# Sketched attention feeding a four-expert layer: two query units a batch instead of three, first k in two halves, dealing strings changed

## The chip, the cores and the metric

The kernel runs on one core of a Trainium2 chip. The metric is device time in microseconds (us) of one execution. All inputs and outputs lie in HBM. TensorE (PE) multiplies matrices, VectorE (DVE), ScalarE (ACT) and GpSimd (POOL) work element by element, and SyncE (SP) issues nearly all DMAs.

## What is computed

For 4 batches, 4 heads, 1088 positions and head size 32, `S1` and `S2` (8 x 32) sketch queries and keys, and the products of the two sketches are the 64 features:

```python
def phi(x):
    a = np.einsum('rd,bhsd->bhsr', S1, x)
    b = np.einsum('rd,bhsd->bhsr', S2, x)
    return np.einsum('bhsi,bhsj->bhsij', a, b).reshape(*x.shape[:-1], r * r)
kv = np.einsum('bhsf,bhsd->bhfd', phi(k), v)
num = np.einsum('bhsf,bhfd->bhsd', phi(q), kv)
den = phi(q) . phi(k).sum(positions) + 1e-6
```

`num / den`, the heads side by side, is a 4352 x 128 matrix `x`. Four experts with `w1` (128 x 1024) and `w2` (1024 x 128) follow: `h = max(x @ w1[e], 0)`, and `out += p[:, e] * (h @ w2[e])`, where `p` is `domain_probs` divided by its row sums.

## The kernel before

**Stream.** The 4352 positions (columns) go through the experts in ten chunks, `CHUNKS` (line 110): 128, 448, six of 512, 320 and 384. For each chunk there are 4 experts x 8 blocks of 128 hidden units. A pair of blocks (chunk 0) or one block (chunks 1 to 9) is a slot, and the main loop (lines 1391 to 1462) writes the program slot by slot. Chunk 0 and experts 0 and 1 of chunk 1 (`WHOLE` = 2) use f32 matmuls directly. Every other block splits both operands into fp32r parts: matmuls L1078 and L1079 into a PSUM tile `h`, an ACT pass over it (L1080), matmul L1095 on top; then element work makes `ha`, `hb`, `hc`; five slots later (`LAG`) L1189 and L1190 multiply `ha` and `hb` by parts of `w2`, and L1224 multiplies `hc`, dealt out after the expert's last block by `DEALT`.

**Makers.** A letter for each block says who makes the parts (lines 1113 to 1146). For all letters but D, ACT makes `ha` (L1119); DVE makes `hb` (L1126) for all. `hc`: A and D, ACT makes a first piece (L1121) and POOL finishes (L1145); P, POOL does both (L1144, L1145); V, DVE alone (L1128); N, ACT makes a whole piece from `ha` and DVE finishes (no POOL). D has DVE make `ha` (L1123). X is a block done in f32 with one row block of `w2` from a small tile `w2_plain`. `MAKER_1` deals chunk 1, `MAKER_LATE[e]` chunks 2 to 9, `MAKER_TAIL` the last expert of chunk 9. `MAKER` is for chunks below `LATE` = 2 other than 1, which have no such block. `BUFFERS` are the numbers of `ha`, `hb` and `hc` tiles.

**Attention.** The generator `front()` (line 989) makes the x columns in pieces, and the main loop takes pieces at a rate that has each chunk ready in time. `keys(b)` (line 539) turns the keys, projects them (L474), copies the values into `vx` (ACT or POOL by `VALUES_BY`), makes products (L498) and sums them over positions on PE (L295). Then come the query units, `UNITS` (line 108). A unit of batches 1 to 3: DVE turns `qn` (L601); PE projects (`project`, 4 matmuls with `sq_half`) and ACT copies; SP writes the result to DRAM (`store_rows`) and reads it back, repeated as the features need it (`spread`); `FETCH` pieces later two products are taken (L790, DVE or POOL by `Q_BY`); 16 pieces after the unit began, `attend` multiplies 64 x 66 tiles on PE, and DVE divides and turns the result (L689 to L707), which goes through DRAM (`xd`) into `ring`, from where `token_parts(m)` splits chunk m.

**Weights.** `weight_parts(e)` and `second_weight_parts(e)` split `w1[e]` and `w2[e]` from the slots in `W1_AT` and `W2_AT`; `W1_BY` and `W2_BY` name the engines (`split` L853 and L855, `rest` L858, `combine` L869).

**Finish.** `gather` (line 1315) adds an expert's gated output to `total`; `TURN` slots after the fourth, DVE turns it (L1289) and SP stores it.

Of the kernel before, what the change touches and what calls it, by code (L numbers as in the profile page):

```python
# [24 lines left out]
def kernel(  # L25
# [35 lines left out]
    NT = 9  # L61
    FB = F // P
    NQ = E * FB // 2
    QW = 512
    CW = 512
    GE = 160
    LAG = 5
    GATES = 3
    BUFFERS = (5, 7, 12)
    HA, HB, HC = BUFFERS  # L70
    WHOLE = 2
    TURN = 2
    MAKER = 'VAXVDDVA'
    LATE = 2
    LATER = 99
    MAKER_1 = 'APXPDPAA'
    MAKER_LATE = ('APVAPAAA', 'APVAPAAA', 'APVPAAAA', 'APVAPAAA')
    TAIL = 4
    MAKER_TAIL = "PAVVXXTT"
    LAG_TAIL = 4  # L80
    MAKER_END = "PAXPAPAA"
    DEALT_TAIL = (1, 1)
    DEALT = (0, 2, 1, 2, 2, 1)
    LIMIT = 1700.0
    LIMIT_A = 1e9
    SLOT_A = 1500.0
    SLOT = 1600.0
    PLAIN = (2,)
    TOKENS_AT = 21
    AHEAD = 13  # L90
    TOKENS = 6
    LEAD = 6
    SETTLE = 1
    SPREAD = 0
    XD_BY = 'VVPPPVPVVV'
    Q_BY = 'VVPPVVPPVVPPVPVPPP'
    O_BY = 'AAAA'
    FETCH = 5
    DELAY = 0
    W1_AT = ((0, 4), (3, 14), (2, 15), (1, 22))  # L100
    W2_AT = ((3, 16), (2, 27), (0, 26), (1, 31))
    W1_BY = ('PVV', 'AVV', 'PVV', 'AVV')
    W2_BY = ('AAPV', 'AAPV', 'APVV', 'AAPV')
    VALUES_BY = 'APA'
    KEYS_BY = "AAA"
    RING_BY = 'PAPA'
    TOKENS_BY = "VV"
    UNITS = [[P, 448, 512], [512, 192, 384], [448, 512, P], [512, 192, 384]]

    CHUNKS = [P, 448] + [512] * 6 + [320, 384]  # L110
    NC = len(CHUNKS)
# [47 lines left out]
    def xpieces(name, t):  # L159
        return mpool.tile([P, 3, CW], t, tag="x", name=name)  # L160

    s_raw = cpool.tile([R2, 2 * D], I32, name="s_raw")
    for i, (eng, src) in enumerate(((nc.scalar, S1), (nc.sync, S2))):
        eng.dma_start(s_raw[R * i : R * i + R, :], src.bitcast(I32))

# [29 lines left out]
        i, c = divmod(P * b, HF)  # L195
        return of[e][i][:, c : c + P]

    load_k(0)
    sr = xpieces("sr", F32)
    qn[0] = mpool.tile([P, 3, CW], F32, tag="x", name="qn_first").rearrange("p i c -> p (i c)")[:, 0:S]  # L200
    load_rows(q, 0, qn[0], slice(0, P))
# [21 lines left out]
        load_w2(e)  # L223
    w2_plain = {}

    def load_plain():

        ((b,),) = (PLAIN,)
        homes = (cpool, "x_first", 0), (mpool, "end", 0), (cpool, "dp", 0), (cpool, "unit", 1)
        for e, (pool, tag, more) in enumerate(homes):  # L230
            w2_plain[e] = pool.tile([P, P + more], F32, tag=tag, bufs=1, name=f"w2_plain_{e}") if pool is mpool else \
                pool.tile([P, P + more], F32, tag=tag, name=f"w2_plain_{e}")
            nc.sync.dma_start(w2_plain[e][:, 0:DM], w2[e, P * b : P * (b + 1), :])

    sk = cpool.tile([P, P], F32, name="sk")
    sp = mpool.tile([32, 3, 2, 32], F32, tag="total", bufs=1, name="sp")
# [63 lines left out]
            on_side(lambda s: out[half[s], :], lambda s: weights[:, half[s]], lambda s: moving, **flags)  # L300


    words = mpool.tile([P, CW], F32, tag="hb", bufs=HB, name="words")

    def word(i, np_=R2):
        return words[0:np_, 2 * D * i : 2 * D * (i + 1)]
# [346 lines left out]
    def attend(b, c, n, qp, after=None):  # L653

        W = H * (D + 1)
        nd = [psum(ps_h, "h")]
        if sum(blocks(m)[0] for _, m in unit_parts(b, c, n)) > 3:  # L660
            nd.append(psum(ps_h, "h"))
        tiles = 0
        laid = []
        for c0, m in unit_parts(b, c, n):
            T = blocks(m)
            for p in range(2):
                for t in range(T[0]):
                    for _ in range(2):

                        at = c0 + P * t + (HP * turn[0] if t < T[turn[0]] else 0)  # L670
                        i, k = divmod(tiles + t, 3)
                        on_side(
                            lambda s: nd[i][half[s], W * k + W // 2 * p : W * k + W // 2 * (p + 1)],
                            lambda s: qp[p][:, at : at + HP],
                            lambda s: kvx[b][:, p, :],
                            start=True,
                            stop=True,
                        )
            laid.append((c0, T, tiles))
            tiles += T[0]  # L680
        if after:
            project(*after)
        yield
        if after:
            store_rows(*after)
        banks = [(i, 3 * i, min(tiles, 3 * i + 3)) for i in range((tiles + 2) // 3)]
        rc = apool.tile([P, QW // 32], F32, tag="rc", name="rc")
        for i, t0, t1 in banks:
            nc.vector.tensor_scalar(  # L689
                out=rc[:, H * t0 : H * t1],  # L690
                in0=_ap(nd[i], 0, P, D, [[D + 1, H * (t1 - t0)]]),
                scalar1=1e-6, scalar2=1.0, op0=ALU.add, op1=ALU.mult,
            )
        nc.vector.reciprocal(rc[:, 0 : H * tiles], rc[:, 0 : H * tiles])
        yield
        xs = apool.tile([P, QW], F32, tag="qa", name="xs")
        for i, t0, t1 in banks:
            nc.vector.tensor_tensor(
                out=_ap(xs, 0, P, P * t0, [[D, H * (t1 - t0)], [1, D]]),
                in0=_ap(nd[i], 0, P, 0, [[D + 1, H * (t1 - t0)], [1, D]]),  # L700
                in1=_ap(rc, 0, P, H * t0, [[1, H * (t1 - t0)], [0, D]]),
                op=ALU.mult,
            )
        yield
        y = apool.tile([P, QW], F32, tag="y", name="y")
        for c0, T, t0 in laid:
            nc.vector.transpose(  # L707
                _ap(y, 0, P, P * t0, [[32, T[0]], [32 * T[0], H], [1, 32]]),
                _ap(xs, 0, P, P * t0, [[P, T[0]], [D, H], [1, D]]),
            )  # L710
            if b == 0 and c == P:
                for x in range(2):
                    yield
                    for a in (x, x + 2):
                        run = 32 * T[a // 2]
                        for h in range(H):
                            copy = scalar_copy if RING_BY[h] == "A" else nc.gpsimd.tensor_copy
                            at = PLACES[1][3] + a // 2 * 64 * T[0] + a % 2 * run
                            copy(ring[32 * h : 32 * h + 32, at : at + run], _ap(y, 32 * a, 32, 32 * T[0] * h, [[1, run]]))
                continue  # L720
            m = 64 * sum(T)
            base = xd.offset + P * (S * b + c + c0)
            for a in range(4):
                run = 32 * T[a // 2]
                nc.sync.dma_start(
                    bass.AP(
                        xd.tensor,
                        base + a // 2 * 64 * T[0] + a % 2 * run,
                        [[m, 32], [32 * m, H], [1, run]],
                    ),  # L730
                    _ap(y, 32 * a, 32, P * t0, [[32 * T[0], H], [1, run]]),
                )
            for to, at, w in placed(S * b + c + c0, m):
                nc.sync.dma_start(to, bass.AP(xd.tensor, base + at, [[m, P], [1, w]]))
        if after and SPREAD == 1:
            spread(*after)
        have[0] += n
        yield
        if after and SPREAD == 2:
            spread(*after)  # L740
# [292 lines left out]
    def final(m, e):  # L1033
        return m == NC - 1 and e == E - 1
# [115 lines left out]
    def second(i):  # L1150
# [25 lines left out]
        elif kind == "one":  # L1176
            w = slice(DM * k, DM * (k + 1))
            va, vb, vd = w2_parts[e]
            last = max(b for b in range(FB) if not plain_block(m, e, b))
            if plain_block(m, e, k):  # L1180
                at = DM * (FB - 1 - k)
                rows = w2_tail[:, at : at + DM] if final(m, e) else w2_plain[e][:, 0:DM]
                if maker(m, e, k) in "YT":
                    weighted.append((rows, hd))
                else:
                    later.insert(len(later) if final(m, e) else 0, (rows, hd))
            else:
                ha, hb, hc = hd
                nc.tensor.matmul(o[:, 0:n], va[:, w], ha, start=(k == first_of(m, e)), stop=False)  # L1189
                nc.tensor.matmul(o[:, 0:n], vb[:, w], hb, start=False, stop=(k == last))  # L1190
                later.append((vd[:, w], hc))
            if final(m, e):
                if k == last:
                    gather_first(m, e, o[:, 0:n])
                    owed.append([0, m, e, psum(ps_h, "h")[:, 0:n], later, DEALT_TAIL])
            elif k == FB - 1:
                if O_BY[e] == "A":
                    nc.scalar.activation(o[:, 0:n], o[:, 0:n], ACTF.Copy, scale=1.0 + R12)  # L1198
                else:
                    nc.vector.tensor_scalar(  # L1200
                        out=o[:, 0:n], in0=o[:, 0:n], scalar1=1.0 + R12, scalar2=1.0, op0=ALU.mult, op1=ALU.mult
                    )
                owed.append([0, m, e, o[:, 0:n], later, DEALT])
# [190 lines left out]
    while i < len(slots) or i <= max(due) or owed:  # L1394
# [34 lines left out]
        if i < len(slots):  # L1429
# [12 lines left out]
                nc.sync.dma_start(bass.AP(one.tensor, one.offset, [[P + 1, P], [1, 1]]), unit[:, P : P + 1])  # L1442
                nc.sync.dma_start(unit[:, 0:P], one[:, :])
            if i == first_slot[1] + 10:
                load_plain()
            if i == first_slot[4]:
                unit = cpool.tile([P, P + 1], F32, tag="unit", name="unit")
                nc.gpsimd.memset(unit[:, 0:P], 0.0)
                nc.gpsimd.memset(unit[:, P : P + 1], 1.0)
            if i == 2:  # L1450
# [45 lines left out]
```

## Time and profile before

| | us |
|---|---|
| runs: median (lowest, highest) | 450.74 (450.14, 451.53) |
| the profiled execution | 451.32 |
| its span, first to last instruction | 449.5 |
| first matmul after the warm-up ones | 6.55 |
| first block of the experts (chunk 0) | 14.23 |
| chunk 1 begins | about 30.7 |
| last weights of the experts used | 441.4 |

The granted TensorE clock is 0.998. A row `start us, us, engine line op out<-in` of the timeline is one instruction or several alike; the bracket behind it is the engine's idle time before it and what ended it. Matmuls are pipelined, so their rows overlap, and the distance of two starts is what one costs.

### The profile page before, as it was taken

How to read it: one execution, taken by the hardware profiler on the slowest of the kernel's cores; microseconds unless marked ns; L12 is line 12 of the kernel's file. 1: busy time of each engine (PE TensorE's matmuls, PEld its weight loads, DVE VectorE, ACT ScalarE, POOL GpSimd, SP SyncE). 2: the span in 40 equal slices, each digit the busy share in tenths (PEclk: the TensorE clock that was granted, in tenths of full speed). 3: DMA queues.
4: the chain of work that ended last, by engine and by line, in shares of the span. 5: the costliest groups of instructions: out<-in, count | busy, mean ns of one | idle time of the engine just before them, and what ended most of it. 6: DMA issues, size and time to landing. Idle time of an engine off the chain costs nothing.

```text
span 449.5 us, 8958 instructions
## 1 busy us (share of the span) xinstructions
PE 440.2 (98%) x2832; PEld 354.7 (79%) x2832; DVE 340.2 (76%) x599; ACT 393.2 (87%) x846; POOL 376.2 (84%) x392
## 2 busy tenths in 40 slices
PE   7999999999999999999999999999999999999996
PEld 6875577878788887877778786787787888999995
DVE  5979968677678779776877669786796768677674
ACT  4257797989999899798989999798999999899992
POOL 5332469989999988899989989898899998999993
PEclk9999999999999999999999999999999999999999
DMA  8906230643331230345403231233300420031100
GB/s 227 307 9 173 63 96 1 121 84 80 124 88 41 59 92 23 90 106 113 133 25 93 46 85 26 71 84 78 80 23 25 107 53 15 23 88 52 32 20 18
DMA packets 48959, 34.54 MB, mean 77 GB/s; under 512 B 25232, under 2 KB 43408, under 8 KB 48912
## 3 DMA queue, kind: packets, MB, share of 16 engines
q1 hardware_dynamic: 48816, 33.87, 29.4%
q8 instruction: 22, 0.36, 0.4%
q14 instruction: 25, 0.20, 0.2%
q10 hardware_dynamic: 96, 0.10, 0.1%
HBM read 28.81 MB, written 5.15 MB: 76 GB/s over the span
## 4 chain that ended last, share of the span: by engine, by line
PE 87%; ACT 4%; DVE 4%; issue 2%; DMA 1%; SPq 0%; DVEq 0%; ACTq 0%
PE h L1078 13%; PE o L1224 13%; PE h L1095 12%; PE h L1079 12%; PE o L1189 12%; PE o L1190 12%; PE h L295 6%; PE h L1071 3%; PE o L1173 3%; ACT ha L1119 2%; ACT h L1080 1%; PE h L474 1%; ACT hc L1121 1%; DMA kn<-in_k_dram 1%; PE o L295 1%
## 5 line engine op out<-in xcount | busy, mean ns | idle before, releaser
L1145 POOL TENSOR_TENSOR hc<-hb,hc 128x512 fp32r<-128x512 f32 (+3 forms) x233 | 288.7, 1263 | 24.1 <-DVE hb L1126 11.4
L1126 DVE SCALAR_TENSOR_TENSOR hb<-h,ha 128x512 fp32r<-128x512 f32 (+3 forms) x266 | 167.9, 641 | 86.3 <-ACT hc L1121 37.9
L1080 ACT ACTIVATE h<-h 128x512 f32<-128x512 f32 (+3 forms) x272 | 165.1, 607 | 6.1 <-PE h L1079 5.4
L1119 ACT ACTIVATE ha<-h 128x512 fp32r<-128x512 f32 (+3 forms) x264 | 159.3, 603 | 4.8 <-PE h L1095 1.2
L1095 PE MATMUL h<-xs,wd 128*128 128x512 f32 (+3 forms) x272 | 105.5, 388 | 0.8 <-ACT h L1080 0.4
L1078 PE MATMUL h<-xs,wa 128*128 128x512 f32 (+3 forms) x272 | 105.0, 386 | 0.2 <-DVE hb L1126 0.2
L1079 PE MATMUL h<-xs,wb 128*128 128x512 f32 (+3 forms) x272 | 102.4, 377 | 0.0
L1189 PE MATMUL o<-ha,va 128*128 128x512 f32 (+3 forms) x266 | 100.7, 379 | 0.9 <-DVE total L1324 0.9
L1190 PE MATMUL o<-hb,vb 128*128 128x512 f32 (+3 forms) x266 | 100.4, 378 | 0.4 <-DVE hb L1126 0.4
L1121 ACT ACTIVATE hc<-h 128x512 fp32r<-128x512 f32 (+3 forms) x164 | 99.1, 604 | 0.2 <-PE o L1224 0.2
L1224 PE MATMUL o<-hc,vd 128*128 128x512 f32 (+3 forms) x262 | 84.5, 383 | 0.0
L1095 PEld LDWEIGHTS h<-xs,wd 128*128 128x128 f32 x272 | 51.1, 188 | 16.2 <-ACT h L1080 6.5
L1078 PEld LDWEIGHTS h<-xs,wa 128*128 128x128 f32 x272 | 51.2, 188 | 11.8 <-issue 2.6
L1189 PEld LDWEIGHTS o<-ha,va 128*128 128x128 f32 x266 | 50.1, 188 | 10.2 <-DVE total L1324 1.6
L1079 PEld LDWEIGHTS h<-xs,wb 128*128 128x128 f32 x272 | 51.3, 188 | 8.4 <-issue 0.4
L1190 PEld LDWEIGHTS o<-hb,vb 128*128 128x128 f32 x266 | 50.0, 188 | 9.6 <-DVE hb L1126 1.1
L1224 PEld LDWEIGHTS o<-hc,vd 128*128 128x128 f32 x262 | 47.9, 188 | 10.5 <-issue 1.5
L1144 POOL TENSOR_SCALAR hc<-ha 128x512 fp32r<-128x512 f32 (+3 forms) x69 | 45.5, 659 | 7.6 <-ACT ha L1119 2.0
L1128 DVE SCALAR_TENSOR_TENSOR hc<-ha,hb 128x512 fp32r<-128x512 f32 (+2 forms) x33 | 32.8, 995 | 1.1
L1198 ACT ACTIVATE o<-o 128x512 f32<-128x512 f32 (+3 forms) x33 | 18.6, 562 | 0.0
L1323 DVE TENSOR_TENSOR o<-o,gate 128x512 f32<-128x512 f32 (+3 forms) x26 | 16.8, 647 | 1.3 <-PE o L1173 1.1
L1324 DVE TENSOR_TENSOR total<-o,total 128x512 f32<-128x512 f32 (+3 forms) x26 | 16.9, 650 | 0.9
(159 smaller groups left out, 394.1 us busy)
## 6 DMA issues: line engine op xcount, KB each, us to landing
w_sb<-in_moe_w_dram SPq DMA_DIRECT2D x8, 512.0 KB
gate<-gates SPq DMA_DIRECT2D x16, 256.0 KB
kn<-in_k_dram SPq DMA_DIRECT2D x4, 544.0 KB
vn<-in_v_dram SPq DMA_DIRECT2D x16, 128.0 KB
gate<-gates SPq DMA_DIRECT2D x8, 224.0 KB
qn<-in_q_dram SPq DMA_DIRECT2D x3, 544.0 KB
qs<-rows SPq DMA_DIRECT2D x6, 256.0 KB
qs<-rows SPq DMA_DIRECT2D x12, 128.0 KB
```

The lines of the kernel that those rows point to most:

```text
L1078: nc.tensor.matmul(g, wa[:, e, w], xa, start=True, stop=False)
L1079: nc.tensor.matmul(g, wb[:, e, w], xb, start=False, stop=True)
L1080: nc.scalar.activation(g, g, ACTF.Copy, scale=1.0 + R12)
L1095: nc.tensor.matmul(g, w, x, start=False, stop=True, skip_group_check=True)
L1119: nc.scalar.activation(ha, g, ACTF.Relu, scale=NEAR)
L1121: nc.scalar.activation(hc, g, ACTF.Relu, scale=NEAR * R12)
L1126: nc.vector.scalar_tensor_tensor(out=hb, in0=g, scalar=0.0, in1=high, op0=ALU.max, op1=ALU.subtract)
L1144: nc.gpsimd.tensor_scalar(out=hc, in0=high, scalar1=R12, scalar2=1.0, op0=ALU.mult, op1=ALU.mult)
L1145: nc.gpsimd.tensor_tensor(out=hc, in0=rest, in1=both_, op=ALU.subtract)
L1189: nc.tensor.matmul(o[:, 0:n], va[:, w], ha, start=(k == first_of(m, e)), stop=False)
L1190: nc.tensor.matmul(o[:, 0:n], vb[:, w], hb, start=False, stop=(k == last))
L1224: nc.tensor.matmul(o, w, h, start=False, stop=True, skip_group_check=True)
```

## The change

Batches 1 to 3 take two units, 576 and 512, where they took three. The tiles that hold a unit grow to 576 (`QW`) or 640 (`XW`) columns; room comes from two `const` tiles (`s_raw` now lies in the tile `words`, and the late `unit` in the place of `dp`). The first k comes as two DMAs of 64 partitions, one from SP and one from ACT. `w2_plain` is loaded six times (before, four times). Numbers and dealing strings change; the entries of `Q_BY` that two units use are the same as before.

```diff
-    QW = 512
+    QW = 576
+    XW = 640
-    BUFFERS = (5, 7, 12)
+    BUFFERS = (5, 5, 14)
-    TURN = 2
-    MAKER = 'VAXVDDVA'
+    TURN = 6
+    MAKER = 'AAXDPPDD'
-    MAKER_1 = 'APXPDPAA'
-    MAKER_LATE = ('APVAPAAA', 'APVAPAAA', 'APVPAAAA', 'APVAPAAA')
+    MAKER_1 = 'APXDPPDP'
+    MAKER_LATE = ('APPAVAAA', 'APVAPAAA', 'APVPAANA', 'APVAPAAA')
-    DEALT_TAIL = (1, 1)
+    DEALT_TAIL = (1, 2)
-    TOKENS_AT = 21
+    TOKENS_AT = 26
-    SPREAD = 0
-    XD_BY = 'VVPPPVPVVV'
-    Q_BY = 'VVPPVVPPVVPPVPVPPP'
+    SPREAD = 1
+    XD_BY = 'VVPPPPPVVV'
+    Q_BY = 'VVPPPPPPVVVPVPVPPV'
-    FETCH = 5
+    FETCH = 8
-    W1_AT = ((0, 4), (3, 14), (2, 15), (1, 22))
-    W2_AT = ((3, 16), (2, 27), (0, 26), (1, 31))
-    W1_BY = ('PVV', 'AVV', 'PVV', 'AVV')
-    W2_BY = ('AAPV', 'AAPV', 'APVV', 'AAPV')
-    VALUES_BY = 'APA'
+    W1_AT = ((0, 4), (2, 14), (3, 17), (1, 24))
+    W2_AT = ((3, 19), (0, 26), (2, 27), (1, 31))
+    W1_BY = ('PVV', 'AVV', 'AVV', 'PVV')
+    W2_BY = ('AAPV', 'AAPV', 'PPPV', 'AAPV')
+    VALUES_BY = 'APP'
-    UNITS = [[P, 448, 512], [512, 192, 384], [448, 512, P], [512, 192, 384]]
+    UNITS = [[P, 448, 512], [576, 512], [576, 512], [576, 512]]
...
-    load_k(0)
+    kn[0] = lpool.tile([P, S], F32, tag="rows", name="kn")
+    for i, eng in enumerate((nc.sync, nc.scalar)):
+        at = slice(HP * i, HP * i + HP)
+        eng.dma_start(kn[0][at, :], bass.AP(k.tensor, k.offset + HP * i * G * D, [[G * D, HP], [1, S]]))
...
+    plain_homes = (cpool, "x_first", 0), (mpool, "end", 0), (cpool, "dp", 0)
+    plain_order = [(m, e) for m in (1, 2) for e in range(WHOLE if m == 1 else 0, E)]
...
             if i == first_slot[1] + 10:
-                load_plain()
+                for j in range(3):
+                    load_plain(j)
+            for j in range(3, len(plain_order)):
+                if i == first_slot[2] + 8 * (j - 3) + 7:
+                    load_plain(j)
```

With `SPREAD` = 1 the read-back of a unit (except a batch's first) is issued after the previous unit's `xd` traffic instead of before it.

More of the change, by code (lines that the diff above doesn't have):

```diff
@@ L160, in xpieces @@
         return mpool.tile([P, 3, CW], t, tag="x", name=name)
-    s_raw = cpool.tile([R2, 2 * D], I32, name="s_raw")
+    words = mpool.tile([P, CW], F32, tag="hb", bufs=HB, name="words")
+    s_raw = words[0:R2, CW - 2 * D : CW].bitcast(I32)
     for i, (eng, src) in enumerate(((nc.scalar, S1), (nc.sync, S2))):
@@ L224, with load_plain @@
     w2_plain = {}
[L226 to L233, printed above, removed]
+    plain_homes = (cpool, "x_first", 0), (mpool, "end", 0), (cpool, "dp", 0)
+    plain_order = [(m, e) for m in (1, 2) for e in range(WHOLE if m == 1 else 0, E)]
+    def load_plain(j):
+        (b,) = PLAIN
+        (pool, tag, more), (m, e) = plain_homes[j % 3], plain_order[j]
+        how = {"bufs": 1} if pool is mpool else {}
+        w2_plain[m, e] = pool.tile([P, P + more], F32, tag=tag, name=f"w2_plain_{j}", **how)
+        nc.sync.dma_start(w2_plain[m, e][:, 0:DM], w2[e, P * b : P * (b + 1), :])
     sk = cpool.tile([P, P], F32, name="sk")
@@ L300, in both @@
             on_side(lambda s: out[half[s], :], lambda s: weights[:, half[s]], lambda s: moving, **flags)
-    words = mpool.tile([P, CW], F32, tag="hb", bufs=HB, name="words")
     def word(i, np_=R2):
@@ L686, in attend @@
         banks = [(i, 3 * i, min(tiles, 3 * i + 3)) for i in range((tiles + 2) // 3)]
-        rc = apool.tile([P, QW // 32], F32, tag="rc", name="rc")
+        rc = apool.tile([P, XW // 32], F32, tag="rc", name="rc")
         for i, t0, t1 in banks:
@@ L695, in attend @@
         yield
-        xs = apool.tile([P, QW], F32, tag="qa", name="xs")
+        xs = apool.tile([P, XW], F32, tag="qa", name="xs")
         for i, t0, t1 in banks:
@@ L704, in attend @@
         yield
-        y = apool.tile([P, QW], F32, tag="y", name="y")
+        y = apool.tile([P, XW], F32, tag="y", name="y")
         for c0, T, t0 in laid:
@@ L1181, in second @@
                 at = DM * (FB - 1 - k)
-                rows = w2_tail[:, at : at + DM] if final(m, e) else w2_plain[e][:, 0:DM]
+                rows = w2_tail[:, at : at + DM] if final(m, e) else w2_plain[m, e][:, 0:DM]
                 if maker(m, e, k) in "YT":
@@ L1444 @@
             if i == first_slot[1] + 10:
-                load_plain()
+                for j in range(3):
[3 more added lines that the diff above has]
+                    load_plain(j)
             if i == first_slot[4]:
-                unit = cpool.tile([P, P + 1], F32, tag="unit", name="unit")
+                unit = cpool.tile([P, P + 1], F32, tag="dp", name="unit")
                 nc.gpsimd.memset(unit[:, 0:P], 0.0)
```

## The prediction, made before the changed kernel had run

> **What bounds the kernel.** I read the page's busy shares first, then its chain of waits.
>
> ```profile
> PE 440.2 (98%) x2832; PEld 354.7 (79%) x2832; DVE 340.2 (76%) x599; ACT 393.2 (87%) x846; POOL 376.2 (84%) x392
> ...
> PE 87%; ACT 4%; DVE 4%; issue 2%; DMA 1%; SPq 0%; DVEq 0%; ACTq 0%
> ```
>
> PE fills the span and 87% of the chain. So time leaves only where PE gets fewer matmuls, starts earlier, or waits less. The timeline gives the price of a matmul, from start to start:
>
> ```profile
> 119.72 0.39 PE L1079 MATMUL h<-xs,wb 128*128 128x512 f32 x1
> 119.96 0.40 PE L1189 MATMUL o<-ha,va 128*128 128x512 f32 x1
> 120.19 0.40 PE L1190 MATMUL o<-hb,vb 128*128 128x512 f32 x1
> ...
> 123.07 0.71 PE L1224 MATMUL o<-hc,vd 128*128 128x512 f32 x2
> 123.70 0.69 PE L295 MATMUL h<-kvx,qs 128*64 128x66 f32 x16
> 124.22 0.82 PE L295 MATMUL h<-qT,sq_half 128*64 128x192 f32 x8
> 124.97 0.50 PE L1078 MATMUL h<-xs,wa 128*128 128x512 f32 x1
> 125.31 0.39 PE L1079 MATMUL h<-xs,wb 128*128 128x512 f32 x1
> ```
>
> A 512-column matmul costs 0.232, a block of six 1.39. The last five rows are an attention interlude: from the second L1224 (123.38) to 125.31 is 1.93, less two matmuls 1.47. I took every distance between big matmuls from 53 to 441 us, less 0.232, 0.203, 0.176 or 0.147 by width and less the small matmuls between: 14 us are left. Some 2.7 of them are the entries and exits of the twelve interludes, the rest waits, in four heaps.
>
> Heap 1, chunk 1's fp32r blocks, 60 to 75 us: about 2.2.
>
> ```profile
> 60.00:65.00 5.00, 4.98 (x21) 3.47 (x19) 3.34 (x7) 5.00 (x13) 4.25 (x5) 1.00 0.18 46
> 65.00:70.00 5.00, 4.79 (x20) 3.52 (x20) 4.97 (x8) 5.00 (x13) 4.75 (x5) 1.00 0.07 16
> 70.00:75.00 5.00, 4.87 (x20) 3.53 (x20) 5.00 (x8) 4.64 (x11) 5.00 (x4) 1.00 0.02 3
> ...
> PEld h L1095 <- ACT h L1080: 2.4, 6, 0.6
> ```
>
> The columns are PE, PEld, DVE, ACT, POOL: ACT is full, and PE's third matmul waits six times for L1080. Heaps 2 and 3:
>
> ```profile
> 92.21 1.81 DVE L790 TENSOR_TENSOR qs<-qs 128x512 f32<-128x512 f32 x1 [2.62 <-DMA qs<-rows]
> ...
> 167.78 2.96 DVE L498 TENSOR_TENSOR kp<-fs 128x512 f32<-128x512 f32 x1
> ...
> 172.72 0.50 PE L1189 MATMUL o<-ha,va 128*128 128x512 f32 x1 [0.92 <-DVE total L1324]
> ```
>
> At 92 DVE stands 2.62 for the read-back of queries, and PE then loses 0.66 on `hb`. At 168 a product that takes 0.68 elsewhere takes 2.96, DVE is late with the gather, and PE loses 1.1 for its bank. Heap 4: 262 to 275, where ACT copies batch 3's values (0.65, 0.66, 0.33), 1.3; and 370 to 420, the narrow chunks, 2.7. The start:
>
> ```profile
> 1.21 4.73 DMA kn<-in_k_dram
> ...
> 5.96 0.46 DVE kp L432
> ...
> 6.55 2.10 PE h L295 x64
> ```
>
> Nothing but k's arrival starts the chain to the first expert block at 14.23; from there PE streams.
>
> **The change, part by part.** PE's expert matmuls are the same in number and form, and so is the order of its last hundred (`DEALT_TAIL` alters nothing there); `MAKER` is read by no block.
>
> *A, fewer units.* Read as above, the four interludes of batch 1 are 3.72, 2.33, 1.93 and 1.51, of batch 2 3.68, 2.62, 1.98 and 1.04, of batch 3 3.79, 2.07, 1.93 and 1.45, each with two big matmuls. Less 8 x 0.232 a batch: 7.64, 7.46, 7.38. Of three: (2.62 - 2.07) / 160 is 3.4 ns a projected column, (1.51 - 1.04) / 16 is 0.029 a 66-column row. With 576 and 512: 3.72 + 0.11 for 32 columns; 2.62 + 8 x 0.029 = 2.86; 1.51 + 0.24 = 1.75; less six matmuls 7.05. Three times: 22.48 - 21.15 = 1.33, of which 0.26 is a wait (2.33 against 2.07 for one shape). I take 1.1.
>
> *B, k in halves.* k is issued at 1.21 and used at 5.94. The DMA view of the first 16 us, in slices of 0.4, shows 121 and 131 GB/s from 2.0 to 2.8, then 304 to 406 until 4.8. If a second queue lets the first two slices run at 350, k is there 0.8 x (350 - 126) / 350 = 0.5 sooner, and I take that. The ends: at most DVE's wait for k, 1.76; at worst -0.2, since ACT's queue needs 0.60 to issue S1 where SP's needs 0.40, so its half starts later. All that comes before 14.23 hangs on k and moves with it; `sk`, ready at 4.7, is late next. [...]
>
> *C, heap 1.* ACT loses two passes an expert in chunk 1 (19 to 17), four in all, and two splits; its passes start 0.49 apart, so about 3. POOL gains two splits (0.80), two `combine` (1.37) and two L1144 (0.64), 5.6; DVE loses two `combine` (0.66), gains two L1123 (0.60). The split and `combine` of expert 2 land where POOL was empty:
>
> ```profile
> 46.00:60.00 14.00, 14.00 (x85) 9.23 (x84) 11.82 (x24) 10.36 (x22) 5.91 (x6) 1.00 0.35 106
> ...
> 60.00:85.00 25.00, 24.63 (x173) 19.05 (x171) 17.82 (x29) 21.65 (x49) 23.49 (x22) 1.00 0.14 35
> ```
>
> 8 us idle before 60, only 1.5 after. Gain 0.8, between -1 (POOL spills) and 2.2.
>
> *D, heap 2.* `FETCH` 8 gives the read-back three more pieces of about 1.3 us, 3.9 against a wait of 2.62 (576 columns, 12% more bytes). Gain 0.7 to 0.9: 0.8, with A's 0.26. For later units `SPREAD` = 1 puts the read-back behind `xd` and ring, whose issue and landing held SP from 53.42 to 56.93; the three pieces pay that back, so 0 there.
>
> *E, heap 3.* `TURN` 6 moves L1289 (0.70) away from the chunk's edge, block 2's V to 4 for expert 0. But POOL still copies batch 2's values beside L498. 0 to 1.1; I take 0.4, nearest the DVE time moved. [...]
>
> *F, heap 4.* Batch 3's values go from ACT to POOL (0.85, 0.85, 0.28): 0 to 1.3, I take 0.7. In 370 to 420 one attention unit less is nearby: 0.2 of 2.7.
>
> *G, the rest.* N for A in expert 2, eight times: POOL -1.35, DVE +0.68 (L1126 reads the same kinds of operands), ACT equal. Fewer stores and loads on SP, two more loads of 64 KB with SP idle: 0. `hb` 7 to 5, `hc` 12 to 14: below. New waits: L790 of 512 takes 0.68 to 1.82, of 576 in proportion 0.77 to 2.05; transposes and divisions 0.15 longer in one piece. Pieces come in bigger lumps, and all of PE's slack was fitted to others. Bounds 0 and -3; I take -0.8.
>
> Sum: 1.1 + 0.5 + 0.8 + 0.8 + 0.4 + 0.9 - 0.8 = 3.7. Against the profiled 451.32: 447.6; this stands 0.58 over the median, so **447.0**.
>
> **Rivals.**
>
> *POOL becomes the bound (slower).* DVE's `hb` waited 9.5 us in ten places for POOL's L1145, with seven tiles; with five, DVE stops two blocks (2.8) sooner, and behind it stand the gathers that free PE's banks. Summing rows over the new order, eight blocks usually hold 10.8 us of POOL work against 11.1 of PE; in chunk 1's last eight 16.6 (before 15.9), at chunk 6's second eight 15.0 (before 12.1). If lag over five blocks reaches PE, it pays that excess, 0.7 + 3.8, and heap 1's spill of 1 to 1.5: 451.3 - 1.6 + 5.7, less 0.6: 454.8. For: these waits. Against: `hc` is used 5 to 13 blocks later, and similar 14.5 before (chunk 4) cost PE nothing. It decides from a lag of about 7 us.
>
> *The waits only move.* A stays, k's halves share one stream, and what C to F free comes back elsewhere: 451.32 - 1.1 - 0.58 = 449.6. For: ACT, DVE and POOL nearly keep their summed durations (ACT -6, POOL -1, DVE 0). If the read-back is not the cause at 92, that is this case too.
>
> *Nearly all waits go.* 1.3 + 1.3 + 5.5 of the waits: 451.3 - 8.1 - 0.6 = 442.6. Against: the narrow chunks keep their makers.
>
> **How the numbers follow.** Forecast 0.58 (444.5 to 449.3 by the terms' ends, likeliest 447.0), waits move 0.17, POOL 0.13, nearly all go 0.12. Faster by over 0.3% (about what a measurement of this kernel can tell from no change) is below 449.4: 0.58 + 0.12. Within: 0.17. Slower, over 452.1: 0.13. The range leaves out POOL's case and the far half of the last: 443.9 to 451.6.
>
> **What would show it.** First matmul at about 6.0 instead of 6.55 (B). Nine interludes, 1.3 less in sum (A). No wait of L790 for `qs` near 92 (D). PE's waits for L1080 in 60 to 75 halved, POOL full there (C). No 0.9 wait for L1324 near 172 (E). Wrong: PE or DVE waiting for POOL's L1145 at chunk 1's end or in chunk 6, or read-backs late for the second units.

## The result, and the profile after

| | before | after |
|---|---|---|
| median of 22 runs each, us | 450.29 (449.74 to 451.53) | 452.04 (450.14 to 453.73) |
| ratio, 95% interval | | 1.003 (1.0017 to 1.0044) |
| the profiled execution, its span | 451.32, 449.5 | 452.12, 450.3 |
| first matmul after the warm-up ones | 6.55 | 6.93 |

The changed kernel is slower by 0.3%, with an interval clear of 1 but about as little as a measurement can tell. I had forecast 447.0, faster, with a range up to 451.6, so the forecast was wrong: the time went the other way and lies 0.4 above the range. The 22 runs of the changed kernel fall in three groups, 450.1 to 450.5 (7 runs), 451.9 to 452.4 (11) and 453.5 to 453.7 (4); what sets them apart is told below.

The page of the changed kernel, in the same order as before:

```profile
PE 440.2 (98%) x2808; PEld 355.7 (79%) x2808; DVE 341.9 (76%) x593; ACT 390.5 (87%) x834; POOL 374.9 (83%) x390
...
PEclk9999999999999999999999989999999999999999
...
PE 81%; DVE 6%; ACT 6%; issue 3%; POOL 2%; DMA 1%; ACTq 0%; DVEq 0%; POOLq 0%
```

PE has 24 matmuls fewer and is as busy. The chain has less of PE (81% for 87%), so more of it passes through other engines. The clock row, all nines before, has one 8, in the 24th of the 40 slices (259 to 270 us).

I followed the two executions slot by slot, by the starts of the experts' matmuls. After minus before: +0.39 at the first block, -0.3 behind chunk 1, -0.78 at 96 us (DVE's wait for `qs` at 92 fell from 2.62 to 0.25), between -0.5 and -1.0 from 159 to 244 us (where no interlude is under way in only one of the two), then **+1.3 from 286 to 302 us** and +2.0 from 311 to 343, +0.3 to +0.65 from 387 us on, +0.88 at the last weights of the experts. So the change did gain where it was to gain, lost 0.4 at the start, and lost 2.0 net between 244 and 286 us, where heap 4 was to give it a gain. (The 0.7 behind 302 us is no wait: the second interlude of batch 3 takes 2.84 where that of the kernel before took 2.07, and there is no fourth.) The start first, in the timeline (start, duration, engine, line, operation):

```profile
1.21 0.57 SPq L203 DMA_DIRECT2D kn<-in_k_dram  x1
1.38 0.56 ACTq L203 DMA_DIRECT2D kn<-in_k_dram  x1
...
6.34 0.77 DVE L438 STREAM_TRANSPOSE kp<-kn 128x256 f32<-128x256 f32 x2 [2.37 <-DMA kn<-in_k_dram]
...
6.93 0.28 PE L302 MATMUL h<-sk,kp 128*64 128x64 f32 x2 [1.30 <-DVE kp L438]
```

k is used at 6.34, not at 5.5. Now the place behind 255 us, the stage in which batch 3's keys and values are made ready:

```profile
255.13 1.08 POOL L448 COPY vx<-vn 128x512 f32<-128x512 f32 x1
...
256.25 0.70 DVE L1295 STREAM_TRANSPOSE ob<-total 128x512 f32<-128x512 f32 x1
...
257.42 0.28 POOL L453 COPY vx<-vn 64x128 f32<-64x128 f32 x1
257.45 3.27 DVE L504 TENSOR_TENSOR kp<-fs 128x512 f32<-128x512 f32 x1
...
257.67 2.51 POOL L1151 TENSOR_TENSOR hc<-hb,hc 128x512 fp32r<-128x512 f32 x2
...
260.65 0.68 DVE L1327 TENSOR_TENSOR total<-o,gate 128x512 f32<-128x512 f32 x1
...
261.38 0.60 PE L1195 MATMUL o<-ha,va 128*128 128x512 f32 x1 [1.85 <-DVE total L1327]
```

Read from below: PE stands 1.85 (2.01 from start to start, less the matmul) for the gather L1327 that frees its bank. The gather is late because DVE was in L504 (L498 in the kernel before), a product of the keys that takes 0.68 alone and took 3.27. While it ran, POOL did its last copy of values (L453), which had begun 0.03 ahead of it, and two L1151 behind that without a gap. And L504 came just behind that copy, and not ahead of it, because DVE had first done L1295, the turn of a finished chunk that `TURN` 6 puts here. So I read these rows; the experiments try it. Then the clock, by stretches (PE, PEld, DVE, ACT, POOL busy, granted clock, DMA):

```profile
258.22:261.63 3.41, 1.56 (x7) 0.99 (x6) 3.41 (x3) 2.28 (x5) 2.90 (x3) 1.00 0.35 59
261.63:265.05 3.42, 3.42 (x9) 2.63 (x9) 3.39 (x5) 1.55 (x3) 2.22 (x2) 0.50 0.56 63
```

Behind the wait the granted clock is 0.50 for 3.41 us: nine matmuls, where the next stretch of this length has sixteen, some 1.7 us lost.

### The profile page after: what moved, and what is told of

Read it like the earlier page. It is cut to its first block, busy times and chain, and to the rows that moved or that the text cites. A ratio compares the mean times of both kernels' runs of the same rounds, so it can differ in the third digit from the quotient of the medians.

```text
span 450.3 us, 8718 instructions
## 1 busy us (share of the span) xinstructions
PE 440.2 (98%) x2808; PEld 355.7 (79%) x2808; DVE 341.9 (76%) x593; ACT 390.5 (87%) x834; POOL 374.9 (83%) x390
## 3 DMA queue, kind: packets, MB, share of 16 engines
HBM read 28.94 MB, written 5.15 MB: 76 GB/s over the span
## 4 chain that ended last, share of the span: by engine, by line
PE 81%; DVE 6%; ACT 6%; issue 3%; POOL 2%; DMA 1%; ACTq 0%; DVEq 0%; POOLq 0%
PE o L1230 12%; PE h L1101 11%; PE h L1084 11%; PE h L1085 11%; PE o L1195 11%; PE o L1196 11%; PE h L302 6%; PE h L1077 3%; PE o L1179 3%; ACT ha L1125 3%; ACT h L1086 1%; PE h L480 1%; ACT hc L1127 1%; POOL hc L1151 1%; DMA kn<-in_k_dram 1%
## 5 line engine op out<-in xcount | busy, mean ns | idle before, releaser
L1151 POOL TENSOR_TENSOR hc<-hb,hc 128x512 fp32r<-128x512 f32 (+3 forms) x225 | 277.4, 1254 | 25.7 <-DVE hb L1132 18.6
L1125 ACT ACTIVATE ha<-h 128x512 fp32r<-128x512 f32 (+3 forms) x262 | 157.6, 602 | 6.8 <-PE h L1101 4.2
L1127 ACT ACTIVATE hc<-h 128x512 fp32r<-128x512 f32 (+3 forms) x154 | 92.8, 602 | 0.0
L1150 POOL TENSOR_SCALAR hc<-ha 128x512 fp32r<-128x512 f32 (+3 forms) x71 | 47.4, 667 | 6.4 <-ACT ha L1125 0.6
L875 POOL TENSOR_TENSOR vd<-va,vb 128x512 fp32r<-128x512 f32 x8 | 11.2, 1408 | 16.3 <-ACT va L859 15.8
## 6 DMA issues: line engine op xcount, KB each, us to landing
gate<-gates SPq DMA_DIRECT2D x16, 256.0 KB
```

What stands on the lines that cost most here:

```text
L1125: nc.scalar.activation(ha, g, ACTF.Relu, scale=NEAR)
L1127: nc.scalar.activation(hc, g, ACTF.Relu, scale=NEAR * R12)
L1150: nc.gpsimd.tensor_scalar(out=hc, in0=high, scalar1=R12, scalar2=1.0, op0=ALU.mult, op1=ALU.mult)
L1151: nc.gpsimd.tensor_tensor(out=hc, in0=rest, in1=both_, op=ALU.subtract)
```

## The experiments

Times are medians. The kernels whose names begin with a, with b or c, and with d were run on three occasions, each beside runs of the kernel before (medians 450.72, 450.32 and 450.71; the changed kernel itself on a fourth, with 450.29). The runs of the kernel before lie near 450.0 or near 450.8, so its median jumps between occasions by 0.4, while its mean stays within 0.15 (450.52, 450.49, 450.63; 450.48). Differences between the medians of two occasions can be off by 0.2 to 0.4. Lines differ by three between kernels with and without the three lines of k's halves: L504 of the changed kernel is L501 there, L1327 is L1324, L1295 is L1292.

My theory after the result: the halves cost 0.4, and POOL's copies of batch 3's values cause the wait at 260 us. The rival: it is `TURN`.

### a1_k_whole

The changed kernel with k in one DMA.

```diff
-    kn[0] = lpool.tile([P, S], F32, tag="rows", name="kn")
-    for i, eng in enumerate((nc.sync, nc.scalar)):
...
+    load_k(0)
```

> The changed kernel with the first k in one DMA from SP, as before. Theory (the halves arrive later, because the second queue's rows start 1.1 us after the first queue's): k is used at about 5.94 instead of 6.32, the first matmul is back at 6.55, and every time falls by 0.4: median about 451.6 against 452.04. Rival (the later arrival is chance of one execution): first matmul stays near 6.9 and the time does not move. Both: the wait of 1.85 us for L1327 near 261 and the slow clock behind it stay.

Measured: 451.09 (0.95 less than with the halves, which ran on another occasion), ratio to before 1.0008 (0.9997 to 1.0018). k is used at 5.48 and the first matmul starts at 6.07. The gain at the start is twice what I expected. The wait at 260 us is still there, and yet in this execution the clock stayed whole behind it:

```profile
257.31:260.72 3.41, 1.58 (x7) 0.94 (x5) 3.41 (x3) 2.56 (x5) 3.19 (x3) 1.00 0.43 74
260.72:264.14 3.42, 3.38 (x15) 2.76 (x16) 3.39 (x4) 2.33 (x5) 2.24 (x2) 1.00 0.47 60
```

PE is as idle in the first stretch as in the changed kernel, 1.58 busy against 1.56, and keeps its clock. So the wait of 2 us and the half clock are two costs, and the second comes in some executions only. (Of the twelve runs, the clock was 0.995 or 0.996 in six.)

### a2_values_apa and a3_turn2

The changed kernel with one constant taken back each, for the theory and for the rival.

```diff
-    VALUES_BY = 'APP'
+    VALUES_BY = 'APA'
```

> The changed kernel with batch 3's values copied by ACT again. Theory (POOL's value copies put POOL behind, its L1151 then come back to back, the product L504 stands behind them for 3 us, the gather is late, PE waits 2 us, and the clock is halved for 3.4 us after it): L504 in batch 3 takes at most 1.8, the wait near 261 is under 0.3, the granted clock is 1.00 until the tail, batch 3's copies on ACT cost up to 1.3 again, and the executions near 452 and 453.6 mostly go: median 450.0 to 450.6. Rival (the bigger lumps of two units and the late turn of L1295 clog DVE): the wait stays over 1 us, median over 451.5.

```diff
-    TURN = 6
+    TURN = 2
```

> The changed kernel with TURN back at 2. Rival (L1295, moved into the key stage by TURN 6, is what makes the gather late): the wait near 261 falls by at least 0.7 to about 1.1, no slow clock, median about 450.3. Theory (the POOL copies do it): the product still takes about 3 us and PE still waits over 1 us near 261; median 451.5 to 452.5.

Measured: 449.37 with batch 3's values on ACT again, ratio 0.9978 (0.9968 to 0.9987); 448.69 with `TURN` 2, ratio 0.997 (0.9957 to 0.9983). Both are below every range that I had given. In both the wait at 260 us is gone. The theory's expectation for `TURN` was wrong: either edit alone removes the wait. With `TURN` 2 the turn lies at 250 us, ahead of the key stage. With the values on ACT it stays in that stage, at 256.52, and POOL does no copies:

```profile
258.06 0.68 DVE L504 TENSOR_TENSOR kp<-fs 128x512 f32<-128x512 f32 x1
...
258.22 1.68 POOL L1151 TENSOR_TENSOR hc<-hb,hc 128x512 fp32r<-128x512 f32 x1 [0.15 <-DVE hb L1132]
```

Here the product began 0.16 ahead of POOL's and took 0.68, and it was POOL's that was held, 1.68 for 1.29. Two of the 12 runs of a2_values_apa and one of the nine of a3_turn2 still have a clock of 0.994 to 0.995 and lie 1.3 to 1.5 above the median, so I take it that a half clock comes in other places too; no profile here shows where.

### a4_k_whole_values_apa and c1_k_whole_turn2

The two pairs, to see whether the gains add.

> Both of the first two: k in one DMA and batch 3's values by ACT. If the two causes are separate they add: median 0.4 below that of the values alone, 449.6 to 450.2, about 0.3 under the kernel before or level with it.

> The changed kernel with k in one transfer and TURN at 2 again. If the two gains add (k whole 0.4 us, TURN 2 without the wait at 259 us): 448.69 less 0.4 or more, 448.0 to 448.4 us, with no wait of TensorE over 1 us from 250 to 270 us. Rival (the gain of k whole at the start is given back at a later wait, as gains before 160 us are taken by the wait at 164): 448.6 to 448.8 us.

Measured: 448.58, ratio 0.9963 (0.9949 to 0.9977), and **447.64**, ratio 0.9941 (0.9929 to 0.9953), five runs within 0.5. They add; both came out below the range expected. The stage of batch 3's keys in c1_k_whole_turn2, with POOL's copies in it, but without the turn:

```profile
256.15 0.88 DVE L501 TENSOR_TENSOR kp<-fs 128x512 f32<-128x512 f32 x1
256.42 0.75 POOL L450 COPY vx<-vn 64x128 f32<-64x128 f32 x1
256.95 0.68 DVE L1324 TENSOR_TENSOR total<-o,gate 128x512 f32<-128x512 f32 x1
257.14 2.55 POOL L1148 TENSOR_TENSOR hc<-hb,hc 128x512 fp32r<-128x512 f32 x2
```

POOL has the same two products in a row, 2.55. But DVE's product starts 0.27 ahead of POOL's last copy and 1 us ahead of them and takes 0.88; it is the copy that is held, 0.75 for 0.28, and the gather follows in time.

### b3_k_halves

The kernel before with k in halves, and nothing else.

```diff
-    load_k(0)
+    kn[0] = lpool.tile([P, S], F32, tag="rows", name="kn")
+    for i, eng in enumerate((nc.sync, nc.scalar)):
...
```

> The kernel before, with its first k fetched as the changed kernel does it, in two halves of 64 rows from SP's and ACT's queues; nothing else is altered. My theory (the halves cost about 0.4 us, since ACT's half starts its packets 1.1 us after SP's): the first matmul starts at about 6.9 us where it was 6.55, and the time is 0.3 to 0.5 us above the kernel before. Rival (the start of the changed kernel is later for another reason, such as the side weights' fetch that moved with the tile words): first matmul at 6.5 to 6.6 and no difference in time.

Measured: 451.44 for 450.32, ratio 1.0029 (1.0014 to 1.0045): 1.1 slower, more than I expected. Its first matmul is at 6.80 in the profile. Over all profiles here, DVE first uses k at 6.20 to 6.37 with the halves (four kernels) and at 5.15 to 5.64 with one DMA (nine), except the profile of the kernel before, 5.96. The row on which I had built the start was thus of a late execution.

### b4_dose

The kernel before, with idle time made for PE: `{3: 5, 4: 6, 5: 7, 6: 8}` products by one added on DVE in the gather of expert 1 of these chunks.

```diff
         g = gate.pop((m, e))[:, 0:n]
+        for _ in range({3: 5, 4: 6, 5: 7, 6: 8}.get(m, 0) if e == 1 else 0):
+            nc.vector.tensor_scalar(out=o[:, 0:n], in0=o[:, 0:n], scalar1=1.0, scalar2=1.0, op0=ALU.mult, op1=ALU.mult)
```

> The kernel before, with 5, 6, 7 and 8 multiplications by one added on VectorE to the gather of expert 1 of chunks 3, 4, 5 and 6, so that TensorE waits there for its bank, a little longer in each chunk; the output is unchanged. Theory (a wait of TensorE of about 2 us can itself bring on the half clock, for some 3.4 us, and this is what makes the groups of times 1.6 us apart): the profile shows waits from about 1 to 3 us, a half clock behind some of those over about 1.8 us and behind none of those under 1 us, and the times fall in groups some 1.6 us apart. Rival (the half clock at 261 us was of something else, such as power or the instant): no half clock behind any of the waits in the profile, and the times lie above the kernel before by the sum of the waits alone, in one group.

Measured: 476.58. The dose was too large: the added products took 0.69 each, and PE's waits came to 4.6, 3.5, 3.9 and 5.0 us where I wanted 1 to 3. All four were followed by a half clock, of 3.413 us in three cases and, behind the wait of 3.5, of 6.827. So idle time does bring it on; how little is enough this run does not tell. What it tells besides: the whole-clock stretches between are 51.2, 51.2, 54.6 and 122.9 us, that is 15, 15, 16 and 36 times 3.413. The one ahead of the half clock in the changed kernel is 256.0, 75 times 3.413. In these two traces the clock changes on a grid of 3.413.

On this grid I summed PE's idle time in every window of the profiles (distances of matmuls, less their cost at full speed). A half clock followed the windows with 2.03 idle (the changed kernel), 2.06 (c2_units_alone, below) and 2.9 or more (four of b4_dose). None followed 2.00 (b4_dose), 1.99 (a1_k_whole) or anything less. The second half-clock window of b4_dose came behind one that was itself at half clock, with six matmuls in it; at full speed these would leave 3.41 - 6 x 0.232 = 2.02 idle, though PE stood for only 0.74 of it. The edge lies at about 2.0 us of 3.41 here, and a wait of 2.0 is just there: where the grid cut it, as in a1_k_whole (1.99), nothing followed. That is argued from these few windows, not tried at the edge. The three groups of the changed kernel's times lie 1.6 apart, as none, one or two such windows would make them; their clocks, 0.999 to 1.0, 0.995 to 0.996 and mostly 0.991 to 0.992, say the same. Only the execution with one such window was profiled, so where the second lies in the slowest group is not known. The window ahead of the half clock in the changed kernel was not wholly idle: PE was busy for 1.56 us of it by the profile.

### d3_values_apa

c1_k_whole_turn2 with batch 3's values on ACT, which fills the square of the two constants.

> The changed kernel with k whole and TURN 2 (447.64 us), and batch 3's values copied by ScalarE as before. My term F (batch 3's values by POOL are worth 0.7 us once TURN 6 does not collide with them): TensorE waits again for some 0.3 to 1 us in 255 to 275 us, and the time is 448.0 to 448.4 us. Rival (values by POOL make VectorE's products long in any order, so that ScalarE is the better engine for them): 447.0 to 447.4 us.

Measured: 448.56, a little above the range. With k whole in all four:

| us | `TURN` 2 | `TURN` 6 |
|---|---|---|
| batch 3's values by ACT (APA) | 448.56 | 448.58 |
| by POOL (APP) | 447.64 | 451.09 |

`TURN` 6 is worth nothing by itself and costs 3.45 beside POOL's copies. POOL's copies are worth 0.92 with `TURN` 2 and cost 2.51 with `TURN` 6. The 447.64 is of the occasion with 450.32; by the ratios to the kernel before, 0.9956, 0.9963, 0.9941 and 1.0008, the 3.45 is 3.0, and the 0.92 is 0.7. Some 0.3 of the 0.92 may be k's arrival, 5.64 in this profile and 5.36 in c1_k_whole_turn2; from 254 to 275 us PE's matmuls fall behind by 0.6, in several small waits.

### d1_fetch5 and d2_chunk1_as_before

c1_k_whole_turn2 with `FETCH` 5, and with `MAKER_1`, `W1_AT`, `W1_BY`, `W2_AT` and `W2_BY` as before.

```diff
-    FETCH = 8
+    FETCH = 5
```

> The changed kernel with k whole and TURN 2 (447.64 us), and FETCH back at 5. My term D (the three more pieces let the read-back of the queries land in time, worth 0.8 us): VectorE's wait for qs near 91 us is 2 to 3 us again, TensorE loses 0.6 or more there, and the time is 448.2 to 448.6 us. Rival (the wait of VectorE is hidden, and what TensorE loses near 96 us comes of the gather in either kernel): the wait of VectorE comes back, but the time stays within 447.4 to 447.9 us.

```diff
-    MAKER_1 = 'APXDPPDP'
+    MAKER_1 = 'APXPDPAA'
...
```

> The changed kernel with k whole and TURN 2 (447.64 us), and chunk 1's makers and the weights' splits with their places as in the kernel before. My term C (work taken from ScalarE in 60 to 75 us is worth 0.8 us): TensorE's losses from 60 to 75 us are back at about 2.2 us, where they are 1.4, and the time is 448.2 to 448.7 us. Rival (POOL or the next stage takes the gain back, so that the dealing of chunk 1 is worth nothing): 447.4 to 447.9 us.

Measured: 449.32 (448.48 to 450.34) and 448.83, so `FETCH` 8 is worth 1.7 and chunk 1's dealing 1.2, both above what I had expected; by the ratios to the kernel before they are 1.5 and 0.9. With `FETCH` 5 the products of the queries are late again:

```profile
92.09 1.61 DVE L793 TENSOR_TENSOR qs<-qs 128x576 f32<-128x576 f32 x1 [0.86 <-DMA qs<-rows]
...
94.36 0.50 PE L1193 MATMUL o<-hb,vb 128*128 128x512 f32 x1 [1.14 <-DVE hb L1129]
```

PE loses 1.3 here, and 0.9 more at 224 us, after DVE has stood 2.38 for the next read-back. (The profiled execution took 450.34, as long as any of the twelve.) The wait of 2 to 3 us that I expected is only 0.86; the product behind it, 1.61, does the rest. In the other kernel, PE's losses from 60 to 75 us are 2.2 (1.4 with the new dealing), and the wait at 96 us is 0.93 (0.48).

### c2_units_alone

The changed kernel with k whole, and `TURN`, `MAKER`, `MAKER_1`, `MAKER_LATE`, `W1_AT`, `W1_BY`, `W2_AT`, `W2_BY`, `VALUES_BY`, `FETCH` and `DEALT_TAIL` as before; `XD_BY`, `Q_BY`, `SPREAD`, `TOKENS_AT` and `BUFFERS` stay as changed.

> The changed kernel's two units a batch with k in one transfer, and with the makers of h, the splits of the weights, their places, the values' engines, TURN and FETCH as in the kernel before. My prediction's terms: fewer units are worth 1.1 us by themselves and the dealing of heaps 1 and 2 is worth the rest, so 449.2 to 450.0 us, with the interludes of batches 1 to 3 at 3.9, 2.85 and 1.75 us and the waits of before at 60 to 75 and at 93 us still there. Rival (the old dealing does not fit the new units, so that new waits eat the gain): 450.3 us or more, with a wait of TensorE at a place where neither kernel has one.

Measured: 452.90, ratio 1.0053 (1.0033 to 1.0073). The rival is right. PE's interludes are as short as in the changed kernel, but there are new waits, 1.8 at 130 us and 2.3 around 224 us with a half clock behind it. Which of the old constants makes each wait was not separated, but for `FETCH`, which by itself made one at 224 us.

### d4_values_aap

c1_k_whole_turn2 with batch 2's values on ACT: the theory of POOL's copies tried at another place.

```diff
-    VALUES_BY = 'APP'
+    VALUES_BY = 'AAP'
```

> The changed kernel with k whole and TURN 2 (447.64 us), and batch 2's values copied by ScalarE, batch 3's still by POOL. Theory (POOL, late from copying the values, runs its products back to back beside VectorE's product of the key stage and holds that up): in batch 2 the 3.8 us product of the key stage falls below 2.5 us, TensorE's wait of 0.67 us near 163 us goes, and the time is 446.8 to 447.2 us. Rival (ScalarE has no room there, as its chain is full in 150 to 165 us): TensorE waits for ScalarE instead, and the time is 447.6 us or more.

Measured: **447.38**, ratio to before 0.9931 (0.9917 to 0.9945), the fastest kernel here, if by 0.26 only, and with an interval that overlaps that of c1_k_whole_turn2. It lies between the two ranges expected. In c1_k_whole_turn2 the key stage of batch 2 has

```profile
157.46 3.79 DVE L501 TENSOR_TENSOR kp<-fs 128x640 f32<-128x640 f32 x1
```

and POOL's three L1148 in a row, 3.78 from 156.79. In d4_values_aap it has

```profile
158.38 1.37 DVE L501 TENSOR_TENSOR kp<-fs 128x640 f32<-128x640 f32 x1
```

The long product is gone and so is PE's wait of 0.67 at 163 us. But ACT, which has the copies now, makes a wait of 0.65 at 149 us. Both had been expected, the first by the theory and the second by the rival.

## Why the prediction was wrong

**The step that failed is E**, "`TURN` 6 moves L1289 (0.70) away from the chunk's edge ... I take 0.4", with F beside it. Each edit was priced against the places of the kernel before, +0.4 and +0.7, and not against where the change puts things. In the kernel before, the turn nearest to heap 3 is this:

```profile
148.08 0.70 DVE L1289 STREAM_TRANSPOSE ob<-total 128x512 f32<-128x512 f32 x1
```

It is 20 us ahead of the product that takes 2.96, so there was no turn for E to move out of the way. And the fewer units, with the numbers that go with them, bring the key stages forward: the first product of batch 3's keys comes at 253.97 where it came at 275.03 (260.52 in c2_units_alone). `TURN` 6 takes the turn from 248.76 to 256.25, which is now inside that stage, and `VALUES_BY` gives POOL its copies there. So three edits meet in one place. By the square above, `TURN` 6 is worth 0.0, POOL's copies 0.6 to 0.9, and both together another -2.7 (by the ratios) to -3.4 (by the medians), a loss outside my range for E (0 to 1.1) and about as large as the worst that I had allowed for G (-3). That `TURN` 6 would have done no harm in batch 3 of the kernel before, where 256.25 is still 19 us ahead of the first product, is argued, not run; nor was the other half of E, the V moved to block 4, tried alone.

The pattern could be seen in the rows that I had quoted, though I took them for POOL's copies: beside the L498 of 2.96 (167.78), POOL has one copy (167.39, 0.28) and then two L1145 in a row (167.64, 2.54), the same three instructions as behind 257.42 in the changed kernel. I did not ask where else the change would put a product of the keys beside such a run of POOL's.

**B failed too, with its sign.** I took +0.5, with -0.2 as its worst. Measured: -0.8 to -1.1 (after against a1_k_whole 0.95, a2 against a4 0.79, a3 against c1 1.05, before against b3_k_halves 1.12). I read the low rate of 2.0 to 2.8 us as room for a second queue; the packets show none. With one DMA (c1_k_whole_turn2) the queue moves 72, 94, 136 and 162 KB in the slices of 0.4 us from 2.2 on, and k's last packet ends at 4.70. With two (the changed kernel), SP's half moves 17, 47, 64 and 128 KB in these slices and ends at 4.21; ACT's half starts only at 3.65 and ends at 5.39, the last of it beside the packets that come next in SP's queue. Why ACT's packets start so late the runs do not show.

E with F, predicted +1.1 and measured -2.5 (448.56 to 451.09), and B, predicted +0.5 and measured about -1, differ by 3.6 and 1.5, about all of the 5.0 by which the forecast missed; the errors of A, C, D and G nearly cancel. The range was also too narrow by its own terms: the ends that I had named for A to G, added, run from about 442 to 453, and the 444.5 to 449.3 that I gave as "the terms' ends" is not their sum.

The other terms held in kind:

| term | predicted | measured |
|---|---|---|
| A, fewer units | 1.1 (1.33 with a wait) | 1.26: the nine interludes of the changed kernel are 25.40 long, less eighteen matmuls 21.22, against 22.48 |
| B, k in halves | 0.5 | -0.8 to -1.1 |
| C, heap 1 | 0.8 | 0.9 to 1.2 |
| D, heap 2 | 0.8 | 1.5 to 1.7, nearly half of it at 224 us in the profiled run |
| E, heap 3, by `TURN` | 0.4 | 0.0 alone, -2.7 to -3.4 more with F |
| F, batch 3's values | 0.7 | 0.6 to 0.9 with `TURN` 2 |

C to F were measured one at a time in c1_k_whole_turn2, so they don't add to its gain: 1.26 + 1.2 + 1.7 + 0.9 is 5.1 (4.3 by the lower figures), and c1_k_whole_turn2 is 2.7 faster than the kernel before. The difference, 1.6 to 2.4, is what G had to hold (-0.8 predicted): I read it so that the old constants fit the new units worse than they fit the old ones (c2_units_alone is slower than the kernel before), so that taking one back costs more than it had gained there; the runs don't divide it further, and `SPREAD`, `TOKENS_AT`, `XD_BY`, `MAKER_LATE` and `BUFFERS` were not tried alone. Heap 3's wait of 1.1 went in all kernels with two units, with `TURN` 2 as with 6, but in all of them but d4_values_aap PE loses 0.63 to 0.68 at 163 to 168 us for it. That 447.64 lies close to my 447.0 is therefore partly chance: C and D were too small, and G too.

Of the rivals, "POOL becomes the bound" named the right engine and the wrong way: five `hb` tiles cost nothing that shows, as d4_values_aap with the same five runs in 447.4. "The waits only move" is nearer to what happened: the largest wait of the kernel before went, and a larger one took its place.

## What to carry to other kernels

When several edits of one change can meet on an engine, first work out where each stage will lie with all of them in place, then list for every stage what that engine will do there; a price against the kernel before holds for one edit alone. Where a product of DVE is near the path, look at whether it starts ahead of POOL's run of instructions: here one that started at 256.15, ahead of POOL's copy at 256.42 (c1_k_whole_turn2), took 0.88, and one at 257.45, just behind the copy at 257.42 (the changed kernel), took 3.27; with k whole on both sides (a1_k_whole for the second, 3.29) the difference was worth about 3. A second queue for one transfer is to be measured and not counted on: here it cost 0.8 to 1.1, and its packets started 1.09 behind those of the first (3.65 and 2.56).

## What the runs showed of the hardware that was not expected

- The granted clock fell to 0.50 for one window of 3.413 us behind a window with 2.03 us of PE idle. If the groups of the times come of it, a wait of 2.0 cost 2.0 in 7 of 22 runs and 3.7 in 11; in 4 a second window was lost, whose place no profile shows. The wait of 1.3 in d1_fetch5 had no half clock behind it.
- A DVE product of the key stage (L504, L501) was held by a run of POOL's instructions and not by one of them only: it took 3.27 beside a copy and two products (0.28 and 2.51), 3.79 beside three products (3.78), against 0.68 to 0.82 alone. It is not always so: another L504 of the same stage of the changed kernel (253.97, 1.76) was held by one L1151 only, until 255.18, and then it was the copy behind it that was held, 1.08 for 0.61. What decides between the two the runs do not show.
- Issuing half of k took 0.57 on SP and 0.56 on ACT, the whole 0.38; ACT's half, issued at 1.38, had its first packet at 3.65, and SP's, issued at 1.21, at 2.56. The whole, issued at 1.21, had it at 2.20.
